# A scan that feeds an expert layer: the first steps, the end of the scan, the gates and the PSUM tiles are reordered

## The chip, the cores and the metric

The kernel runs on one core of a Trainium2 chip. The metric is the device time of one execution in microseconds. The engines are called by the names that the profile uses: PE (TensorE, with its weight loads as PEld), DVE (VectorE), ACT (ScalarE), POOL (GpSimd) and SP (SyncE, which issues most DMAs). A lower time is better.

## The reference

Two layers follow one another. The first is a scan with decay over 768 positions of 4 sequences with 8 heads (head size 32, state size 16), in chunks; the second sends each of the 3072 resulting rows of 256 numbers to one of 8 experts.

```
for each chunk of the sequence:
    L  = exp(cum_i - cum_j), causal            # cum = cumulative sum of log(a) inside the chunk
    y  = ((C B^T) * L) x  +  exp(cum) * (C state)
    state = exp(sum log a) * state + sum_j exp(cum_last - cum_j) * B_j x_j
x = y as [3072, 256]
logits = (x/|x|) . (emb/|emb|) / tau           # cosine router, 8 experts
gate   = softmax(logits)[argmax]
out[r] = gate[r] * relu(x[r] w1[e]) w2[e],  e = argmax(logits[r])   # w1: 256x1024, w2: 1024x256
```

## The kernel before, in words

The order in which the program is written is the order of each engine's queue (`manual_schedule`): nothing is moved afterwards. Engines wait for one another through semaphores only where one needs what another makes, or a buffer that another still uses. PSUM, into which PE writes, has eight banks; the kernel names them `pgA`, `pgB`, `py` (two banks each) and `pz0`, `pz1` (one each) and uses the same five tiles in the scan and in the experts.

**The scan** works on 6 chunks of 128 positions, and on each in two steps of two sequences, so there are 12 steps. Ahead of them `decays` (DVE) makes the decay factors, `spread_decays` (L214, PE) copies those of a chunk from 32 rows to all the rows that need them, by a product with a 0/1 matrix, and ACT brings them to SBUF as `fr`; `inverse` and `turn_inverse` make the reciprocals `rT`. `embeddings` norms the experts' vectors (L268) and `turn_embeddings` turns them. A step is made of `scores` (L430: C times the decay, `cp`, against B, split by `split_b` into the two heads of a row group, `bz`, L157 on ACT), `masks` (a copy on ACT, L440, a product on DVE, L441, a selection on POOL, L447), `outputs` one step later (L462 from the state, L471 from the scores), `tokens` another step later (L520: the row and its logits), and `keep_tokens` (ACT copy to `yt`, L531, and a DMA to the table `rows` in HBM). Every second step makes the new state (`sums`, `states`). `scale_c` (DVE) and `scale_x` (POOL, for the first chunk DVE) prepare a chunk ahead.

**The routing** runs beside it, per chunk: `pick` finds the expert of each token, `ranks` counts by small products where each comes in its expert's list, `places` makes two 0/1 patterns `low` and `hv` from it (L367), and `table` and `keep_table` (L374, L383) add to a table of row numbers per expert. Of expert 0 the first 256 rows are taken from chunks 0 to 3 alone, so `early_rows` can gather them before the scan has ended; it issues the gather of job 0 (L637, on POOL).

**The experts** are nine jobs: job 0 (256 early rows of expert 0), job 1 (160 more), jobs 2 to 8 (416 rows each, experts 1 to 7). A job is a gather of its rows (L637; four instructions for 416 rows), `turn_x` (transposes L675 and copies L677), eight `up` (L685: 2 products each, 4 instructions in the profile; relu by turns on ACT L689 and DVE L691), `gates` (squares on ACT L655, a pow on POOL L658, five short steps on DVE, an exp on ACT L662), `down` (L699: two halves of 8 products each, 16 instructions in the profile; copies on ACT L703 and DVE L705) and `out` (transposes L713, scaling by the gate on ACT L719 and DVE L717, scatter L720 on POOL). `up` takes three banks in turn, the input transposes one, `down` two, the output transposes two. The jobs overlap by one: `out` of job n stands behind the second `up` of job n+1, and the gather of job n+2 behind `down` of job n. In job 4 `left_blocks` (L809 to L860, mostly DVE) computes where rows beyond 416 would go; there are none, and `leftover` runs no loop.

Of the kernel before, what the change touches and what calls it, by code (L numbers as in the profile page):

```python
# [7 lines left out]
F32 = mybir.dt.float32  # L8
# [38 lines left out]
def early_consts(k):  # L47
# [5 lines left out]
    g.iota(head_i[:], pattern=[[NH, NB], [1, 4], [4, 2], [0, N]], base=0, channel_multiplier=0)  # L53
    v.memset(k.a0[64:128, 1, :], 1.0)
# [98 lines left out]
def split_b(k, c):  # L153
    t = k.ld[c]
    t.bz = k.work.tile([128, 2, NB, Q], F32, name="bz", tag="bz")
    for v in range(2):
        k.nc.scalar.activation(t.bz[:, v], t.bt[:], ACT.Copy, scale=k.tmask[:, v : v + 1])  # L157
# [9 lines left out]

def decays(k):  # L170
# [23 lines left out]
    v.tensor_tensor(out=k.f[:, :, HQ], in0=w[:, 0], in1=at[:, :, 0], op=ALU.mult)  # L194

# [10 lines left out]
def spread_at(k, c):  # L206
    return (k.py[:, 0], k.py[:, 1], k.pz[0], k.pz[1], k.pgA[:, 0], k.pgA[:, 1])[c]


def spread_decays(k, c):  # L210
    g = 32 * (c % 4)
    ps = spread_at(k, c)
    for b in range(NB):
        k.nc.tensor.matmul(  # L214
            ps[:, 128 * b : 128 * b + 128], lhsT=k.spread[g : g + 32, b, :], rhs=k.f[g : g + 32, c // 4, :],
            start=True, stop=True, tile_position=(g, 0),
        )
# [39 lines left out]
def embeddings(k):  # L257
# [7 lines left out]
    nc.scalar.dma_start(tau[:], k.tau.to_broadcast([E, 1]))  # L265
    sq = k.mc.tile([E, DM], F32, name="emb_sq")
# [13 lines left out]
def turn_embeddings(k, ps):  # L280
# [5 lines left out]
    nc.vector.tensor_copy(out=k.turn[:, 0, LG : LG + E], in_=ps[:, 0:E])  # L286
    nc.vector.tensor_copy(out=k.turn[:, 1, 0:E], in_=ps[:, E : 2 * E])
# [18 lines left out]
def ranks(k, c):  # L306
    nc = k.nc
    ob = k.ob[c]
    at = k.pz[1][:, AT : AT + NB * E].rearrange("p (b e) -> p b e", b=NB)
# [10 lines left out]
    if c in (3, NC - 1):  # L320
        n = k.pz[1][:, CNT : CNT + E]
# [48 lines left out]
def table(k, c):  # L370
    nc = k.nc
    ps = k.pz[0][:, TB : TB + 2 * E * NT]
# [6 lines left out]
def keep_table(k, c):  # L379
    nc = k.nc  # L380
    ps = k.pz[0][:, TB : TB + 2 * E * NT]
    acc = k.acc[:].rearrange("p v m -> p (v m)")
    nc.vector.tensor_tensor(out=acc, in0=acc, in1=ps, op=ALU.add)  # L383
# [142 lines left out]
def keep_tokens(k, p):  # L526
    nc = k.nc
    c, b, _ = pair(k, p)
# [8 lines left out]
def mamba(k):  # L537
# [3 lines left out]
    early_consts(k)  # L541
    load(k, 0)
# [7 lines left out]
    for c in (0, 4, 5, 1, 2, 3):  # L550
        spread_decays(k, c)
    flat = lambda c: k.fr[:, c].rearrange("p b m -> p (b m)")
    nc.scalar.copy(out=flat(0), in_=spread_at(k, 0))
    nc.vector.memset(k.fr[:, 0, :, HQ], 1.0)
    nc.scalar.copy(out=k.fr[:, 4:6].rearrange("p c b m -> p c (b m)"), in_=k.pgA[:])
    scale_c(k, 0)
    scale_c(k, 1)
    inverse(k, 0)
    scores(k, 0)
    for c in (1, 2, 3):  # L560
        nc.scalar.copy(out=flat(c), in_=spread_at(k, c))
    turn_inverse(k, 0, k.py[:, 0, 0:128])
    k.rT = k.mc.tile([128, 2, 128], F32, name="rT")
    nc.scalar.copy(out=k.rT[:, 0], in_=k.py[:, 0, 0:128])
    scale_x(k, 0, nc.vector)
    scale_x(k, 1, nc.vector)
    masks(k, 0)
    inverse(k, 1)
    between(k)
    turn_inverse(k, 1, k.py[:, 0, 0:128])  # L570
    nc.scalar.copy(out=k.rT[:, 1], in_=k.py[:, 0, 0:128])
    turn_embeddings(k, k.pz[0])
    split_b(k, 1)
    scale_c(k, 2)
    load(k, 2)

    for s in range(1, NP + 2):
# [13 lines left out]
        if s % 2 and s >= 5:  # L591
# [406 lines left out]
```

## Time and profile before

| | |
|---|---|
| median of 3 runs | 373.27 us (370.19 to 374.04) |
| the profiled execution | 374.36 us, of which the trace spans 372.6 us |
| mean granted clock of PE | 0.917 |
| busy | PE 289.9, PEld 181.1, DVE 115.4, ACT 84.3, POOL 105.7 us |
| start to the first scores of step 2 | 25.14 us |
| from there to the scores of step 11 | 45.64 us |
| from there to the first matmul of job 2 | 69.94 us |
| from there to the first `down` product of job 8 | 204.11 us |
| the rest | 27.77 us |

The time of an execution is 1.76 us more than its span here. The page gives busy times of the whole span; the stretches are read with the view by windows, which gives busy times and the clock of PE for each. In a group or timeline row, the number in brackets is how long the engine stood still ahead of the instruction, and the name behind `<-` is what released it. In the waits view a row has the total, the times and the longest. A matmul that is written once appears as two instructions in the profile, since the numbers are float32.

### The profile page before, as it was taken

Reading aid. Unit: us, or ns where it says so; the run is one execution under the profiler, and the core shown is the slowest. Engines: PE = TensorE matmul, PEld = TensorE weight load, DVE = VectorE, ACT = ScalarE, POOL = GpSimd, SP = SyncE. Lnnn points to the kernel's source line nnn. Section 1 sums busy time; section 2 is a strip of 40 time slices with the busy share of each in tenths; the row PEclk is TensorE's granted clock in tenths of the full one; section 3 lists DMA queues with packets and bytes.
Section 4 is the critical chain, followed back from the end, with each engine's and each line's share of the span. In section 5 each row is a group of like instructions: output and inputs, shape, how many; then the busy total and the mean of one; then the engine's idle time right before and its main releaser. Section 6 shows DMA issues by size and latency. Waiting matters only on the chain.

```text
span 372.6 us, 5520 instructions
## 1 busy us (share of the span) xinstructions
PE 289.9 (78%) x2159; PEld 181.1 (49%) x2159; DVE 115.4 (31%) x356; ACT 84.3 (23%) x210; POOL 105.7 (28%) x130
## 2 busy tenths in 40 slices
PE   3777879857549689798889799497988996898940
PEld 3666768744327675344345354234444453454420
DVE  3476767861320312302211220812033023122010
ACT  3445555530100203101301300130031022013010
POOL 4334453430420523401800810260035022014030
PEclk9999999995857969989999899869999999999995
DMA  6506692831110144503232230413043240001010
GB/s 212 221 4 201 203 360 99 270 107 29 32 27 0 43 140 131 155 3 113 73 125 90 85 130 0 128 59 131 0 151 82 83 138 14 0 0 46 0 41 7
DMA packets 20428, 34.76 MB, mean 93 GB/s; under 512 B 2232, under 2 KB 13700, under 8 KB 20400
## 3 DMA queue, kind: packets, MB, share of 16 engines
q1 hardware_dynamic: 17360, 27.94, 22.1%
q0 software_dynamic: 2816, 6.40, 5.8%
q8 instruction: 17, 0.28, 0.3%
q14 instruction: 11, 0.09, 0.1%
q10 hardware_dynamic: 224, 0.06, 0.1%
HBM read 28.26 MB, written 6.65 MB: 94 GB/s over the span
## 4 chain that ended last, share of the span: by engine, by line
PE 59%; issue 10%; DVE 7%; ACT 7%; POOL 4%; DMA 2%; POOLq 0%; DVEq 0%; ACTq 0%
PE py L699 23%; PE pgA L685 16%; PE pgB L685 6%; PE pgB L675 3%; PE py L471 2%; PE pz L520 2%; ACT hT L689 2%; PE pgA L430 2%; DVE hT L691 2%; POOL gr L658 2%; PE pz L713 2%; PE py L462 1%; POOL out_dram L720 1%; DVE xT L677 1%; ACT bz L157 1%
## 5 line engine op out<-in xcount | busy, mean ns | idle before, releaser
L699 PE MATMUL py<-hT,w 128*128 128x416 f32 (+2 forms) x288 | 99.0, 500 | 5.0 <-ACT yoT L703 5.0
L685 PE MATMUL pgA<-xT,w 128*128 128x416 f32 (+2 forms) x192 | 79.6, 543 | 25.8 <-ACT hT L689 21.7
L699 PEld LDWEIGHTS py<-hT,w 128*128 128x128 f32 x288 | 55.1, 202 | 44.4 <-issue 32.5
L720 POOL DMA_INDIRECT out_dram<-yo,to x30 | 29.2, 975 | 165.7 <-ACT yo L719 155.4
L685 PEld LDWEIGHTS pgA<-xT,w 128*128 128x128 f32 x192 | 37.8, 215 | 59.0 <-ACT hT L689 31.7
L637 POOL DMA_INDIRECT xg<-rows,table x30 | 30.1, 1002 | 21.3 <-DVE to_u L402 13.2
L685 PE MATMUL pgB<-xT,w 128*128 128x416 f32 (+2 forms) x96 | 35.9, 499 | 0.0
L705 DVE COPY yoT<-py 128x416 f32<-128x416 f32 (+2 forms) x9 | 4.9, 543 | 99.2 <-PE py L699 87.7
L691 DVE TENSOR_SCALAR hT<-pgA 128x416 f32<-128x416 f32 (+2 forms) x24 | 12.9, 536 | 57.0 <-PE pgA L685 47.2
L689 ACT ACTIVATE hT<-pgA 128x416 f32<-128x416 f32 (+2 forms) x24 | 11.5, 478 | 67.8 <-PE pgA L685 67.8
L685 PEld LDWEIGHTS pgB<-xT,w 128*128 128x128 f32 x96 | 18.9, 205 | 13.1 <-issue 12.7
L447 POOL TENSOR_SCALAR_AFFINE_SELECT g<-g 128x1024 f32<-128x1024 f32 x12 | 13.5, 1123 | 37.4 <-ACT g L440 35.8
L675 PE MATMUL pgB<-ident,xg 128*128 128x128 f32 x64 | 13.7, 309 | 11.8 <-DVE xT L677 6.1
L703 ACT COPY yoT<-py 128x416 f32<-128x416 f32 (+2 forms) x9 | 4.2, 467 | 80.2 <-PE py L699 80.2
L430 PE MATMUL pgA<-cp,bz 32*128 32x128 f32 x192 | 16.9, 313 | 6.4 <-ACT bz L157 5.2
L675 PEld LDWEIGHTS pgB<-ident,xg 128*128 128x128 f32 x64 | 8.6, 155 | 19.8 <-DVE xT L677 7.3
L430 PEld LDWEIGHTS pgA<-cp,bz 32*128 32x128 f32 x192 | 13.7, 209 | 8.2 <-ACT bz L157 7.0
L430 PE MATMUL pgB<-cp,bz 32*128 32x128 f32 x192 | 16.9, 312 | 0.0
L713 PE MATMUL pz<-ident,yoT 128*128 128x128 f32 (+1 forms) x64 | 10.9, 285 | 7.6 <-DVE yo L717 4.5
L441 DVE TENSOR_TENSOR g<-pgA,mask 128x1024 f32<-128x1024 f32 x12 | 14.6, 1216 | 2.4 <-PE pgB L430 2.4
L520 PE MATMUL pz<-turn,yT 128*128 128x136 f32 x96 | 14.6, 293 | 0.1
L440 ACT COPY g<-pgB 128x1024 f32<-128x1024 f32 x12 | 12.1, 1006 | 8.6 <-PE pgB L430 7.5
(184 smaller groups left out, 294.0 us busy)
## 6 DMA issues: line engine op xcount, KB each, us to landing
w<-in_moe_w_dram SPq DMA_DIRECT2D x16, 1024.0 KB, 5.6
rows<-yt SPq DMA_DIRECT2D x12, 264.0 KB, 3.7
x<-in_x_dram SPq DMA_DIRECT2D x6, 512.0 KB, 5.5
ct<-in_CT_dram SPq DMA_DIRECT2D x6, 256.0 KB, 3.0
bt<-in_BT_dram SPq DMA_DIRECT2D x6, 256.0 KB, 4.2
b<-in_B_dram SPq DMA_DIRECT2D x6, 256.0 KB, 6.5
xg<-rows,table POOLq DMA_INDIRECT x30, 2.8
out_dram<-yo,to POOLq DMA_INDIRECT x30, 2.4
```

Of the source, the lines that this page charges most:

```text
L430: k.nc.tensor.matmul((k.pgA, k.pgB)[q // 2][:, q % 2, a : a + 128], lhsT=t.bz[r, v, b + i, :], rhs=t.cp[r, b + i, :], start=True, stop=Tru ...
L441: nc.vector.tensor_tensor(out=s.g[:, 0:2].rearrange("p q a i -> p (q a) i"), in0=k.pgA[:].rearrange("p q (a i) -> p (q a) i", a=4), in1=bc ...
L447: nc.gpsimd.affine_select(out=g, in_=g, pattern=[[0, 8], [1, Q]], compare_op=ALU.is_ge, fill=0.0, base=0, channel_multiplier=-1)
L520: k.nc.tensor.matmul(k.pz[i][:, at : at + Y1], lhsT=yT[:, j, i, :], rhs=k.turn[:, j, :], start=(j == 0), stop=(j == 1), skip_group_check=True,
L637: s.k.nc.gpsimd.indirect_dma_start(out=s.x[0:p, i, 0:TOK], out_offset=None, in_=rows, in_offset=bass.IndirectOffsetOnAxis(ap=s.at[0:p, i : ...
L675: nc.tensor.transpose(t[:, o : o + p], s.x[0:p, i, Y1 * j : Y1 * j + 128], k.ident[:p, :p])
L685: nc.tensor.matmul(t, lhsT=s.w1[:, j, 128 * f : 128 * f + 128], rhs=s.xT[:, j, :], start=(j == 0), stop=(j == KD - 1))
L689: nc.scalar.activation(s.hT[:, f, :], t, ACT.Relu)
L691: nc.vector.tensor_scalar_max(s.hT[:, f, :], t, 0.0)
L699: nc.tensor.matmul(t, lhsT=s.w2[:, f, 128 * j : 128 * j + 128], rhs=s.hT[:, f, :], start=(f == 0), stop=(f == KF - 1))
L713: nc.tensor.transpose(t[:p, 128 * j : 128 * j + 128], s.yT[:, j, o : o + p], k.ident[:])
L720: d = nc.gpsimd.indirect_dma_start(out=k.out[:, :], out_offset=bass.IndirectOffsetOnAxis(ap=s.to[0:p, i : i + 1], axis=0), in_=y[:p], in_o ...
```

## The change

The change has five parts.

1. **First steps.** A tile of zeros and a first `Square` on ACT come at the very start; nine products with zeros (`fill`) stand on PE ahead of and behind the first spread. The spread of chunks 0 to 3 goes over the four row groups in turn (chunk within block, where it was block within chunk), that of chunks 4 and 5 comes after the scores of step 0. `scale_c` of the first two steps reads PSUM. Norm and turn of the embeddings come after the masks of step 0, their copies go from DVE to ACT, and the second `inverse` moves to steps 3 and 4. The scores and masks of steps 0 and 1 are written out in `begin_scan`.
2. **B split sooner.** `split_b` of the next chunk moves from the odd step to the even step before it.
3. **End of the scan.** `table(3)`, its addition and `early_rows` move into step 11: the products behind the scores, the rest behind the masks. The last steps are written out.
4. **Experts.** Eight tiles of one bank each come from a pool of their own, with `reuse_waits="tile"`. `gates` is split into `squares` (with the pow) and the rest; for job n+1 both stand between the two halves of `down` of job n, and the gather of job n+2 between them. `left_blocks` stands in front of the second half of `down` of job 4. In job 0 the relus of `up` 0 to 5 are all on ACT, and `gates` and the gathers are reordered.
5. **A drain** of POOL stands behind the scatter of job 7, in the last expert.

The core of the diff:

```diff
+def fill(k, n):
+    for _ in range(n):
+        k.nc.tensor.matmul(k.pgB[:, 1, 0:Q], lhsT=k.zero[:, 0:Q], rhs=k.zero[:, Q:], start=True, stop=True)
...
-def spread_decays(k, c):
-    g = 32 * (c % 4)
-    ps = spread_at(k, c)
+def spread_decays(k, chunks):
     for b in range(NB):
...
+        for c in chunks:
+            g = 32 * (c % 4)
...
-    for c in (0, 4, 5, 1, 2, 3):
-        spread_decays(k, c)
...
+    spread_decays(k, range(4))
     inverse(k, 0)
+    fill(k, 1)
+    turn_inverse(k, 0, k.pgB[:, 1, 0:128])
...
+    keep_decays(k, 1)
...
+    scale_c(k, 0, spread_at(k, 0))
     scores(k, 0)
...
+    scale_c(k, 1, spread_at(k, 0))
     scale_x(k, 0, nc.vector)
+    keep_decays(k, 2)
+    masks(k, 0)
+    spread_decays(k, (4, 5))
+    keep_decays(k, 4)
+    keep_decays(k, 5)
     scale_x(k, 1, nc.vector)
...
+    scores(k, 1)
+    keep_decays(k, 3)
     between(k)
...
+    norm_embeddings(k)
+    masks(k, 1)
     turn_embeddings(k, k.pz[0])
...
             scores(k, s)
+            if s == NP - 1:
+                table(k, 3)
             masks(k, s)
...
+            if s == NP - 1:
+                keep_table(k, 3)
+                early_rows(k)
...
+        if s % 2 == 0 and s // 2 + 1 < NC:
+            split_b(k, s // 2 + 1)
...
-        if s % 2 and c + 1 < NC and s > 1:
-            split_b(k, c + 1)
...
+    def squares(s):
...
+        nc.gpsimd.tensor_tensor(out=s.r[:], in0=s.r[:], in1=k.half[:, 0:nt], op=ALU.pow)
...
+    banks = [k.ps.tile([128, 512], F32, name=f"bank{i}") for i in range(8)]
+    k.bank = {"hp": ring(banks[0:3]), "xt": ring(banks[3:4]), "yp": ring(banks[4:6]), "ot": ring(banks[6:8])}
...
+    j0.up(6)
+    j0.up(7)
+    load_weights(k, 2)
+    j0.down(0)
+    j0.squares()
     begin(1)
     j0.gates()
...
+    j0.down(1)
     jobs[1].turn_x()
...
+    jobs[1].squares()
+    jobs[1].gates()
     for n in range(1, E + 2):
...
                 jobs[n - 1].out()
-            if f == 3 and n <= E:
-                jobs[n].gates()
+                if n == E:
+                    k.nc.gpsimd.drain()
         if n + 1 <= E:
             jobs[n + 1].turn_x()
         if n <= E:
-            jobs[n].down()
+            jobs[n].down(0)
+        if n + 1 <= E:
+            jobs[n + 1].squares()
         if 2 <= n + 1 < E:
             begin(n + 1)
+        if n + 1 <= E:
+            jobs[n + 1].gates()
+        if n == E // 2:
+            left_blocks(k)
+        if n <= E:
+            jobs[n].down(1)
```

Line numbers move: the scores are L430 before and L453 after, the table's products L374 and L397, the relu on ACT L689 and L740, the squares L655 and L695, the exp L662 and L713, the pow L658 and L699, the gather L637 and L684, the scatter L720 and L772.

Three places show how the instructions stand. The first is PE at the end of the scan: the last scores (step 11), and what follows them. Before:

```order
L430 MATMUL pgA<-cp,bz 128x128 x2
L430 MATMUL pgB<-cp,bz 128x128 x2
L462 MATMUL py<-cp,T 32x128 x16
L471 MATMUL py<-g,xs 32x128 x16
L520 MATMUL pz_74<-turn,yT 128x136 x2
L520 MATMUL pz_75<-turn,yT 128x136 x2
L374 LDWEIGHTS low
L374 MATMUL pz_74<-hv,low 128x64
```

After:

```order
L453 MATMUL pgA<-cp,bz 128x128 x2
L453 MATMUL pgB<-cp,bz 128x128 x2
L397 LDWEIGHTS low
L397 MATMUL pz_87<-hv,low 128x64
L397 LDWEIGHTS low
L397 MATMUL pz_87<-hv,low 128x64
L397 LDWEIGHTS low
L397 MATMUL pz_87<-hv,low 128x64
L397 LDWEIGHTS low
L397 MATMUL pz_87<-hv,low 128x64
L485 MATMUL py<-cp,T 32x128 x16
```

The table's products of chunk 3 (`hv`, `low`) have moved from behind the outputs and tokens of step 10 to the place right behind the scores; the outputs (L462, now L485) stand behind them.

The second is ACT in an expert. Here `hT<-` are the relus of `up`, `yoT<-` is the copy of the first half of `down`, `yo<-` the output scaling, and the `bank_` numbers are the eight one-bank tiles (1372 to 1374 for `up`, 1376 for the first half of `down`, 1378 for the outputs). Before, an expert from the output scaling to the next job's first relu:

```order
L719 ACTIVATE yo<-pz_74,gate 128x256 x2
L689 ACTIVATE hT<-pgA 128x416
L655 ACTIVATE sq,gr<-xg_179 128x256 x4
L662 ACTIVATE gl<-gl 128x32
L689 ACTIVATE hT<-pgA 128x416
L689 ACTIVATE hT<-pgB 128x416
L703 COPY yoT<-py 128x416
L689 ACTIVATE hT<-pgA 128x416
```

After:

```order
L771 ACTIVATE yo<-bank_1378,gate 128x256 x2
L740 ACTIVATE hT<-bank_1374 128x416
L740 ACTIVATE hT<-bank_1373 128x416
L740 ACTIVATE hT<-bank_1372 128x416
L755 COPY yoT<-bank_1376 128x416
L695 ACTIVATE sq,gr<-xg_181 128x256 x4
L713 ACTIVATE gl<-gl 128x32
L740 ACTIVATE hT<-bank_1374 128x416
```

The squares and the exp (`gl`) stood between two relus of the same job. Now they are the next job's, behind the copy of the first half of `down`, and the next relu is the first of the next job.

The third is POOL at the first jobs: gathers (`xg`), pows (`gr`) and scatters (`out_dram`). Before:

```order
L637 DMA xg_178<-rows,early_i 128x264 x2
L637 DMA xg_179<-rows,table 128x264
L637 DMA xg_179<-rows,table 32x264
L637 DMA xg_180<-rows,table 128x264 x3
L637 DMA xg_180<-rows,table 32x264
L658 TENSOR_TENSOR gr<-gr,half 128x2
L720 DMA out_dram<-yo,early_to 3072x256 x2
L658 TENSOR_TENSOR gr<-gr,half 128x2
```

After:

```order
L684 DMA xg_180<-rows,early_i 128x264 x2
L684 DMA xg_181<-rows,table 128x264
L684 DMA xg_181<-rows,table 32x264
L699 TENSOR_TENSOR gr<-gr,half 128x2
L684 DMA xg_182<-rows,table 128x264 x3
L684 DMA xg_182<-rows,table 32x264
L699 TENSOR_TENSOR gr<-gr,half 128x2
L772 DMA out_dram<-yo,early_to 3072x256 x2
```

The pow of job 0 has moved ahead of the four gathers of job 2; that of job 1 stands behind them and ahead of the scatter of job 0.

More of the change, by code (lines that the diff above doesn't have):

```diff
@@ L150, in load, with split_b @@
     nc.sync.dma_start(t.b[:].rearrange("p b m -> p (b m)"), k.B[c])
-def split_b(k, c):
+def split_b(k, c, halves=(0, 1)):
     t = k.ld[c]
-    t.bz = k.work.tile([128, 2, NB, Q], F32, name="bz", tag="bz")
-    for v in range(2):
+    if 0 in halves:
+        t.bz = k.work.tile([128, 2, NB, Q], F32, name="bz", tag="bz")
+    for v in halves:
         k.nc.scalar.activation(t.bz[:, v], t.bt[:], ACT.Copy, scale=k.tmask[:, v : v + 1])
@@ L651, in gates @@
         )
-        r = k.p.tile([128, nt], F32, name="gr", tag="gr")
-        for i in range(nt):
-            sq = k.p.tile([128, 2, 128], F32, name="sq", tag="sq")
-            nc.scalar.activation(
-                sq[:], x[:, i].rearrange("p (j w) -> p j w", j=2)[:, :, 0:128], ACT.Square, accum_out=r[:, i : i + 1],
-            )
-        nc.gpsimd.tensor_tensor(out=r[:], in0=r[:], in1=k.half[:, 0:nt], op=ALU.pow)
         nc.vector.tensor_scalar_add(r[:], r[:], 1e-6)
@@ L691, in up, with down @@
             nc.vector.tensor_scalar_max(s.hT[:, f, :], t, 0.0)
-    def down(s):
+    def down(s, j):
         k, nc = s.k, s.k.nc
-        s.yT = k.p.tile([128, KD, s.w], F32, name="yoT", tag="yoT")
-        for j in range(KD):
+        if j == 0:
+            s.yT = k.p.tile([128, KD, s.w], F32, name="yoT", tag="yoT")
+        for j in (j,):
             t = k.bank["yp"]()[:, 0 : s.w]
@@ L937 @@
     k.route = ctx.enter_context(tc.tile_pool(name="route", bufs=2))
-    ps = ctx.enter_context(tc.tile_pool(name="ps", bufs=1, space=PSUM))
-    k.pgA = ps.tile([128, 2, 512], F32, name="pgA")
-    k.pgB = ps.tile([128, 2, 512], F32, name="pgB")
-    k.py = ps.tile([128, 2, 512], F32, name="py")
-    k.pz = [ps.tile([128, 512], F32, name=f"pz{i}") for i in range(2)]
     k.yt = k.const.tile([128, NU, TOK], F32, name="yt")
@@ L950 @@
             k.mc = m.enter_context(tc.tile_pool(name="mc", bufs=1))
+            ps = m.enter_context(tc.tile_pool(name="ps", bufs=1, space=PSUM))
+            k.pgA = ps.tile([128, 2, 512], F32, name="pgA")
+            k.pgB = ps.tile([128, 2, 512], F32, name="pgB")
+            k.py = ps.tile([128, 2, 512], F32, name="py")
+            k.pz = [ps.tile([128, 512], F32, name=f"pz{i}") for i in range(2)]
             mamba(k)
         k.p = ctx.enter_context(tc.tile_pool(name="moe", bufs=2, reuse_waits="tile"))
+        k.ps = ctx.enter_context(tc.tile_pool(name="moe_ps", bufs=1, space=PSUM, reuse_waits="tile"))
         moe(k)
```

181 lines of the change are left out of this document (99 added, 82 removed).

## The prediction

> **What bounds the kernel now.** I read the page first, then stretches of the span, then the waits, then the timeline where the long waits lie. The page:
>
> ```profile
> PE 289.9 (78%) x2159; PEld 181.1 (49%) x2159; DVE 115.4 (31%) x356; ACT 84.3 (23%) x210; POOL 105.7 (28%) x130
> PEclk9999999995857969989999899869999999999995
> ```
>
> TensorE (PE) is busy for 78% of the span. The rest is 82.7 us in which it waits, and some of the busy time is matmuls at the half clock (the fives in the second row). So I ask of each stretch how long PE stands and at which clock. The columns are length, busy time of PE, PEld, DVE, ACT and POOL, the granted clock, DMA share and GB/s. The cuts are at the first scores of step 2 (25.14), those of step 11 (70.78), the first transpose of job 0 (85.10), the end of its long stall (106.53), the first matmul of job 2 (140.72), and then the first down matmul of jobs 4 (220.09), 5, 6, 7 and 8.
>
> ```profile
> 0.00:25.14 25.14, 15.21 (x180) 14.04 (x180) 11.19 (x39) 9.97 (x17) 7.96 (x33) 1.00 0.46 161
> 25.14:70.78 45.64, 38.25 (x1073) 32.32 (x1066) 34.09 (x84) 26.05 (x47) 23.43 (x23) 1.00 0.59 201
> 70.78:85.10 14.32, 8.63 (x202) 7.13 (x198) 8.85 (x41) 5.13 (x12) 3.89 (x4) 0.90 0.54 181
> 85.10:106.53 21.43, 11.43 (x40) 7.62 (x41) 5.78 (x27) 2.33 (x9) 6.60 (x7) 0.66 0.11 28
> 106.53:140.72 34.19, 28.90 (x121) 23.20 (x122) 6.25 (x22) 3.63 (x13) 6.83 (x7) 0.76 0.15 50
> 220.09:258.14 38.05, 29.93 (x82) 15.10 (x81) 12.09 (x42) 5.34 (x16) 8.98 (x9) 0.87 0.27 87
> 258.14:288.22 30.08, 26.31 (x82) 13.38 (x81) 6.15 (x17) 5.22 (x16) 9.00 (x9) 1.00 0.27 84
> 288.22:317.95 29.73, 25.43 (x81) 13.62 (x81) 6.34 (x17) 5.22 (x16) 4.99 (x5) 1.00 0.22 81
> 344.83:372.60 27.77, 12.92 (x41) 6.61 (x39) 2.14 (x4) 1.45 (x3) 3.88 (x4) 0.81 0.05 16
> ```
>
> The expert rows are bound by PE (25.4 of 29.7 us); the rows from 70.78 to 140.72 are not, and run at 0.66 to 0.90 of the clock. The waits view names what PE stands for (total us, times, longest):
>
> ```profile
> PE pgA L685 <- ACT hT L689: 21.7, 15, 8.1
> PE py L699 <- ACT yoT L703: 5.0, 9, 0.6
> PE pgA L430 <- ACT bz L157: 5.2, 4, 1.4
> ```
>
> An up matmul waits for the relu that frees its PSUM bank; ScalarE (ACT) is late with the relu because the gate's exp is ahead of it in its queue, and that waits for VectorE (DVE), which waits for the pow on GpSimd (POOL). The timeline of job 0 shows the whole chain, the worst of its kind:
>
> ```profile
> 103.67 0.91 POOL L637 DMA_INDIRECT xg<-rows,table  x1 [0.30 <-issue]
> 104.61 0.74 POOL L658 TENSOR_TENSOR gr<-gr,half 128x2 f32<-128x2 f32 x1
> 105.99 0.21 ACT L662 ACTIVATE gl<-gl 128x16 f32<-128x16 f32 x1 [10.11 <-DVE gl L661]
> 106.53 2.07 PE L685 MATMUL pgA<-xT,w 128*128 128x256 f32 x4 [8.13 <-ACT hT L689]
> ```
>
> The pow stands behind the last of six gathers (five of them at 0.30 us from the one before), and PE loses 8.13 us.
>
> **The change, part by part.** *Start.* Timeline rows:
>
> ```profile
> 5.62 2.07 PE L214 MATMUL py<-f,spread 32*128 32x128 f32 x8 [5.62 <-DVE f L194]
> 5.76 1.28 ACT L268 ACT_TABLE_LOAD   x1 [5.76 <-DMA tau<-in_moe_tau_dram]
> 11.88 2.08 PE L214 MATMUL pz<-f,spread 32*128 32x128 f32 x12
> 12.16 0.58 ACT L553 COPY fr<-py 128x512 f32<-128x512 f32 x1 [3.37 <-PE py L214]
> 13.72 0.58 PE L430 MATMUL pgA<-cp,bz 32*128 32x128 f32 x2
> ```
>
> The decays are ready at 5.62, but the spread of chunks 0, 4, 5, 1, 2, 3 runs chunk after chunk to 12.16, and the copy for `scale_c` waits for it. Before, twelve products on mixed row groups took 2.08 us; the sixteen for chunks 0 to 3, now dealt over four groups, should take no more than 2.1, so they end at 7.7. The table load no longer waits for tau, so the first B halves are done by then, and `scale_c` reads PSUM without the copy (0.58). With 0.4 us for it scores(0) start at 8.3, 5.4 sooner than 13.72. From there to scores(2) 11.4 us passed (to 25.14). New ACT copies (chunks 1, 2, 4, 5, 3 one by one, the turn table) and the embedding chain, which now stands between the first two steps, can take some of it back. I take −4.5, with bounds −2 (the chain becomes late) and −6.5 (the distance shrinks too). The nine fill products are before 5.6, where PE had nothing.
>
> *Scan.* Four stalls of 1.4 us for `bz` (5.2 in all) go, because the split is issued a step sooner, ahead of its use by about five us. DVE is next: it is busy 34.1 of 45.6 us and the chain mask, scale, states is late by about as much. I take −1.5, bounds 0 and −3.
>
> *End of the scan, jobs 0 and 1 (70.78 to 140.72, 69.94 us).* PE's work at the full clock is 8.63×0.90 + 11.43×0.66 + 28.90×0.76 = 37.3 us. It stood 69.94 − 48.96 = 21.0 us. What remains of that: the gather of job 0 hung on keep_table(3), which moves ahead of outputs(10):
>
> ```profile
> 81.41 1.32 POOL L637 DMA_INDIRECT xg<-rows,early_i  x1 [5.54 <-DVE early_to_u L403]
> 85.15 0.47 PE L675 MATMUL pgB<-ident,xg 128*128 128x128 f32 x1 [3.87 <-DMA xg<-rows,early_i]
> 73.41 0.40 ACT L367 ACTIVATE hv<-hi,part 128x128 bf16<-128x128 f32 x1 [2.13 <-DVE hi L360]
> ```
>
> The `hv` of chunk 3 is ready at 73.8; with the products (0.3), the add after the mask on DVE (to 75.1) and the indices (0.4) the gather goes out about 75.9, 5.5 sooner. The wait for `hv` now also holds outputs(10) for up to 1.5 us, so the transposes come only 3.8 sooner: 5.7 − 3.8 = 1.9 us stay in the first row. In the second the 8.13 goes, since pow of job 0 is now ahead of the four gathers of job 2 and relus 0 to 5 ahead of the exp: 10.0 − 8.1 = 1.9 stay. What is late next is job 1: its exp waits for a pow behind those four gathers (1.3 us apart, 5.2), of which about 3.6 lie beside down(1) and the transposes; 1.6 is left, and 1.6 of small waits in the third row. Sum 7.0, so 44.3; I add 2.6 for one or two half-clock windows (next part). 46.9, thus −23.0. Bounds: −27 at the full clock and with no stall in job 1; −17 if its stall is the whole 5.2 and two more windows are half.
>
> *Experts 2 to 8 (140.72 to 344.83, 204.11 us).* Rows of one undisturbed expert:
>
> ```profile
> 294.60 5.85 PE L699 MATMUL py<-hT,w 128*128 128x416 f32 x16 [0.60 <-ACT yoT L703]
> 300.29 1.56 PE L685 MATMUL pgB<-xT,w 128*128 128x416 f32 x4
> 303.08 0.60 PE L713 MATMUL pz<-ident,yoT 128*128 128x128 f32 x4
> 304.55 1.56 PE L685 MATMUL pgA<-xT,w 128*128 128x416 f32 x4
> 306.56 0.41 ACT L655 ACTIVATE sq<-xg 128x256 f32<-128x256 f32 x1
> ...
> 311.51 1.66 PE L685 MATMUL pgA<-xT,w 128*128 128x416 f32 x4 [2.61 <-ACT hT L689]
> 315.81 0.66 PE L675 MATMUL pgB<-ident,xg 128*128 128x128 f32 x4
> 317.23 0.72 PE L675 MATMUL pgB<-ident,xg 128*128 128x128 f32 x4 [0.75 <-DVE xT L677]
> 317.88 2.36 PE L699 MATMUL py<-hT,w 128*128 128x416 f32 x6
> ```
>
> By starts: half of a down 5.69 (294.60 to 300.29), one up 1.39 (two from 300.29 to 303.08), the output transposes 1.47 (to 304.55), the input transposes 2.07 (315.81 to 317.88). Without the 2.61 (gates) and the 0.60 (second half waits for the copy of the first, which before shared a two-bank tile) a period is 2×5.69 + 8×1.39 + 1.47 + 2.07 = 26.1. The gates' cover is now the second half of down: after the copy (0.5) come four squares (4×0.41), the pow (0.74 in job 0, for half the columns; I take 1.0), three short DVE steps and the exp (0.21): with the hand-overs about 3.8 us, under 5.69. If that slips by over 2 us, the next relu is late by the rest. The block table (L809 to L860, on DVE) keeps its price: the row at 220.09 is 38.05 − 30.08 = 8.0 longer, and as its step now stands ahead of the copy of the second half, the output transposes still wait for it, by 4 us or so. Bounds 3.7 (the wait alone) and 9. Six periods less the transposes that job 8 doesn't issue: 154.6; up to the first down of job 2 (8 ups, two output blocks, transposes) 14; the block table 8; one half-clock window 1.7. Sum 178.3, so −25.8, bounds −19 and −28.
>
> The clock has rows of its own:
>
> ```profile
> 153.90:157.30 3.40, 2.03 (x10) 1.19 (x10) 1.48 (x3) 0.00 (x0) 0.00 (x0) 1.00 0.65 172
> 157.30:160.70 3.40, 3.40 (x6) 1.69 (x5) 0.30 (x1) 0.00 (x0) 0.00 (x0) 0.50 0.34 140
> ```
>
> A stretch of 3.4 us in which PE was busy for 2.0, 1.45 of them in the eight transposes of job 3, was followed by one at half, which costs 1.7. [...]
>
> *Tail.* The first scatter of the last job, and the drains at the kernel's end (count, shortest, median and longest in ns, first and last start):
>
> ```profile
> 358.91 1.05 POOL L720 DMA_INDIRECT out_dram<-yo,to  x1 [19.05 <-ACT yo L719]
> L994 POOLq DRAIN  x3: 46/107/5301, 366.5 to 372.4; - x3
> ```
>
> One drain of 5.30 us runs near the end, from 366.5, and two others take 0.11 and 0.05. The early drain stands where POOL is idle for 19.05 us, waiting for the last job's outputs, so it costs nothing there. If its price belongs to what was queued since the start, or to the first drain, the last falls to the level of the other two: −5.0. If it belongs to the last scatters, 0. Both ends stay in the range; I take −5.0, nearer the rows of the two cheap drains. With the 0.6 of down: −5.6.
>
> Sum: 372.6 − 4.5 − 1.5 − 23.0 − 25.8 − 5.6 = 312.2. The profiled execution took 374.36, 1.76 more than its span, so 314; it lies 1.1 above the median 373.27, which gives 313.
>
> **The rivals.** *Half clock more often.* With fewer waits the transposes (2.07 and 1.47 us per expert) become the thin places; if every expert from 2 to 8 has one half window, that adds six more, 6×1.7 = 10, so 323. For: 157.30, where transposes alone did it. Against: the row at 288.22 has the same transposes, and a wait of 2.61, at 1.00. [...]
>
> *The last drain stays.* +5: 318. For: it is what POOL does behind the last scatters, and theirs could be the cost. Against: POOL issues one of these in 1.05 us, and 5.30 for four of them that are under way already would be more than their issue took.
>
> *The gates' wait moves.* If pow is late (ACT's squares and the scatters are in front of it), the exp holds relu 0 of the next expert, by what it was before: 7×2.6 = 18, so 331.
>
> *Start and scan give nothing, DVE being the bound:* 313 + 6 = 319, and with the bound of the middle (6 less) 325.
>
> *Slower.* The same queue, at its worst: the exp of job n+1 stands ahead of relu 0 on ACT and its DVE steps ahead of the copy of the second down half. If x of n+1 or the pow came as late as in job 0, PE would lose 8.13 plus 3.4 of half clock behind it, 11.5 per expert, 81 in all: 394. It decides from 60/7 = 8.6 per expert. Against: the gathers of n+1 are now issued a whole expert ahead, and four gathers take 5.2, not 7.8.
>
> **How the numbers follow.** Forecast as summed 0.42; half clock 0.18; drain stays 0.16; gates move 0.08; start and scan give nothing 0.10; slower 0.03; about no change, several of these together, 0.03. The likeliest gives 313. The low end, 303, takes the good bounds of the middle and the experts (−4, −2.2) and most of the start's and scan's (−3.5); the high end, 331, takes in all rivals but the last two cases, and the bound of the middle. Within 1%, about what a measurement of this kernel can tell from no change, is 369.5 to 377: 0.03; slower 0.03; faster 0.94.
>
> **What would show it.** Scores(2) at 19 to 22 us; no wait for `bz` over 0.5; the first gather 5 us after scores(11); no PE wait over 3 us between job 0 and job 2; expert periods of 26 to 27 with no wait of L685's line for ACT over 1 us and none of the down line; the clock row at 9 through the experts except the block table; the drain near the end under 1 us, and one of about 5 us at the last expert where POOL waits. The forecast is wrong if the periods stay at 29, if pow is late again, or if the five in the clock row come with every expert.

## The result, and the profile after

The changed kernel takes 314.25 us in the median of four runs (310.73 to 315.82), against 373.14 before: a ratio of 0.840, with a 95% interval of 0.832 to 0.847. The forecast was 313, with a range of 303 to 331. Ratios, here and below, are taken from the faster of two states into which the executions of a kernel fall, so they can differ a little from the quotients of the medians. The page of its profiled execution (314.79 us, span 313.1), as far as it answers to the rows shown of before:

```profile
PE 270.8 (87%) x2177; PEld 178.2 (57%) x2177; DVE 115.2 (37%) x352; ACT 86.3 (28%) x217; POOL 105.8 (34%) x130
PEclk9558999995999799999999999779999999999997
L736 PE MATMUL bank<-xT,w 128*128 128x416 f32 (+2 forms) x288 | 96.7, 489 | 2.0 <-ACT hT L740 2.0
L751 PE MATMUL bank<-hT,w 128*128 128x416 f32 (+2 forms) x288 | 91.7, 476 | 0.0
```

The last two rows are the up and down products; what stands behind the second bar is PE's idle time ahead of them: 2.0 us and none, where the waits for the relu alone were 21.7 and those for the first down half 5.0. The clock row has no fives left in the experts; three stand elsewhere, two in the start and one at the end of the scan. The stretches, cut at the same events as before (scores of step 2 at 21.26, of step 11 at 70.00, first matmul of job 2 at 115.49, first down product of job 8 at 292.00; two single experts between):

```profile
0.00:21.26 21.26, 14.13 (x198) 12.82 (x198) 12.42 (x40) 10.03 (x20) 10.66 (x35) 0.71 0.54 191
21.26:70.00 48.74, 40.78 (x1066) 34.26 (x1066) 33.20 (x85) 26.63 (x48) 21.32 (x20) 0.95 0.58 194
70.00:115.49 45.49, 40.09 (x359) 34.25 (x359) 20.43 (x88) 13.43 (x44) 12.90 (x13) 0.89 0.29 93
115.49:292.00 176.51, 163.17 (x518) 90.11 (x517) 46.98 (x138) 34.77 (x102) 57.12 (x58) 0.98 0.30 94
155.04:180.97 25.93, 24.90 (x82) 13.79 (x81) 6.27 (x17) 5.35 (x16) 9.01 (x9) 1.00 0.35 110
180.97:216.23 35.26, 27.08 (x82) 14.79 (x81) 12.19 (x42) 5.36 (x16) 9.17 (x10) 0.90 0.27 84
292.00:313.10 21.10, 12.65 (x41) 6.72 (x39) 2.14 (x4) 1.45 (x3) 3.82 (x4) 0.91 0.06 21
```

| stretch | before | after | difference | forecast |
|---|---|---|---|---|
| start to scores of step 2 | 25.14 | 21.26 | −3.9 | −4.5 |
| to scores of step 11 | 45.64 | 48.74 | **+3.1** | −1.5 |
| to the first matmul of job 2 | 69.94 | 45.49 | −24.5 | −23.0 |
| to the first down product of job 8 | 204.11 | 176.51 | −27.6 | −25.8 |
| to the end | 27.77 | 21.10 | −6.7 | −5.6 |

The sum is −59.5, the forecast was −60.4. The scan went the other way. The first rows of the two kernels can't be compared by their clocks: before, the row reads 1.00, but the scores of steps 0 and 1 take 2.16 and 2.17 us in it, and 1.17 in step 2; after, they take 2.09 where the trace has the clock at 0.50 (9.11 to 26.18 us). Two further things in the trace were not as the terms had them. The expert with the block table is 35.26 long, 9.3 more than its neighbour. Its timeline:

```profile
195.28 0.17 POOL L870 IOTA step_i<- 128x32 int32 x1
195.48 0.18 DVE L872 CAST step_f<-step_i 128x32 f32<-128x32 int32 x1 [3.85 <-POOL step_i L870]
202.03 0.58 DVE L757 COPY yoT<-bank 128x416 f32<-128x416 f32 x1
202.66 2.16 PE L765 MATMUL bank<-ident,yoT 128*128 128x128 f32 x7 [7.36 <-DVE yoT L757]
```

The first instruction of the table is a small iota on POOL, which now stands behind the four gathers of job 6. DVE waits 3.85 us for it, and the copy of the second down half, with PE behind it, waits for the whole. The granted clock is 0.50 from 200.25 to 207.08, around the end of this wait.

And the scan's waits of PE (total, times, longest; whole span):

```profile
PE py L494 <- issue: 4.2, 3, 1.7
PE pgA L453 <- DVE g L464: 2.3, 3, 1.0
```

The 5.2 us for `bz` are gone; in their place are waits for the mask on DVE, and 4.2 us in which PE waited for nothing that the profile shows (0.95 before).

### The profile page after: what moved, and what is told of

It reads as the page before. It is cut to its first block, busy times and chain, and to the rows that moved or that the text cites. A ratio compares the mean times of both kernels' runs of the same rounds, so it can differ in the third digit from the quotient of the medians.

```text
span 313.1 us, 5513 instructions
## 1 busy us (share of the span) xinstructions
PE 270.8 (87%) x2177; PEld 178.2 (57%) x2177; DVE 115.2 (37%) x352; ACT 86.3 (28%) x217; POOL 105.8 (34%) x130
## 4 chain that ended last, share of the span: by engine, by line
issue 55%; PE 17%; POOL 16%; DVE 8%; ACT 1%; POOLq 1%; DMA 1%; ACTq 0%; DVEq 0%
POOL out_dram L772 8%; POOL xg L684 7%; PE py L494 4%; PE pz L543 3%; PE pgA L453 3%; PE bank L736 2%; PE py L485 1%; DVE g L464 1%; DVE cp L253 1%; DVE T L533 1%; PE py L225 1%; PE pz L512 1%; DMA a<-in_a_dram 1%; POOL gr L699 1%; ACT fr L232 1%
## 5 line engine op out<-in xcount | busy, mean ns | idle before, releaser
L736 PE MATMUL bank<-xT,w 128*128 128x416 f32 (+2 forms) x288 | 96.7, 489 | 2.0 <-ACT hT L740 2.0
L751 PE MATMUL bank<-hT,w 128*128 128x416 f32 (+2 forms) x288 | 91.7, 476 | 0.0
L736 PEld LDWEIGHTS bank<-xT,w 128*128 128x128 f32 x288 | 54.5, 199 | 37.4 <-issue 33.7
L751 PEld LDWEIGHTS bank<-hT,w 128*128 128x128 f32 x288 | 52.5, 190 | 34.9 <-issue 33.7
L772 POOL DMA_INDIRECT out_dram<-yo,to x30 | 29.2, 974 | 42.5 <-ACT yo L771 35.5
L742 DVE TENSOR_SCALAR hT<-bank 128x416 f32<-128x416 f32 (+2 forms) x33 | 18.3, 554 | 63.0 <-PE bank L736 60.8
L699 POOL TENSOR_TENSOR gr<-gr,half 128x4 f32<-128x4 f32 (+1 forms) x9 | 8.7, 972 | 95.7 <-ACT sq L695 95.7
L684 POOL DMA_INDIRECT xg<-rows,table x30 | 30.2, 1008 | 21.6 <-DVE to_u L425 13.5
L740 ACT ACTIVATE hT<-bank 128x416 f32<-128x416 f32 (+2 forms) x39 | 18.1, 470 | 65.1 <-PE bank L736 60.4
L453 PE MATMUL pgA<-cp,bz 32*128 32x128 f32 x192 | 17.0, 326 | 5.0 <-DVE cp L253 2.7
L494 PE MATMUL py<-g,xs 128*32 128x128 f32 x384 | 16.9, 313 | 4.2 <-issue 4.2
L765 PE MATMUL bank<-ident,yoT 128*128 128x128 f32 (+1 forms) x64 | 11.4, 298 | 10.2 <-DVE yoT L757 7.9
L453 PEld LDWEIGHTS pgA<-cp,bz 32*128 32x128 f32 x192 | 14.4, 225 | 6.3 <-DVE g L464 2.7
L726 PE MATMUL bank<-ident,xg 128*128 128x128 f32 x64 | 11.5, 273 | 6.6 <-DVE xT L728 6.1
L453 PE MATMUL pgB<-cp,bz 32*128 32x128 f32 x192 | 17.1, 328 | 0.0
L494 PEld LDWEIGHTS py<-g,xs 128*32 128x32 f32 x384 | 12.0, 124 | 7.8 <-issue 7.5
```

What stands on the lines that cost most here:

```text
L453: k.nc.tensor.matmul((k.pgA, k.pgB)[q // 2][:, q % 2, a : a + 128], lhsT=t.bz[r, v, b + i, :], rhs=t.cp[r, b + i, :], start=True, stop=Tru ...
L494: nc.tensor.matmul(k.py[g : g + 32, v, 128 * i : 128 * i + 128], lhsT=t.xs[:, b + i, 4 * v + q, :], rhs=s.g[:, q, 2 * i + v, :], start=(c ...
L684: s.k.nc.gpsimd.indirect_dma_start(out=s.x[0:p, i, 0:TOK], out_offset=None, in_=rows, in_offset=bass.IndirectOffsetOnAxis(ap=s.at[0:p, i : ...
L736: nc.tensor.matmul(t, lhsT=s.w1[:, j, 128 * f : 128 * f + 128], rhs=s.xT[:, j, :], start=(j == 0), stop=(j == KD - 1))
L740: nc.scalar.activation(s.hT[:, f, :], t, ACT.Relu)
L742: nc.vector.tensor_scalar_max(s.hT[:, f, :], t, 0.0)
```

## The experiments

Twelve kernels were run, in three groups, each beside runs of the kernel before on the same chip (medians 374.3, 376.0 and 374.0). Ratios are to those runs; the changed kernel has 0.840.

**1. No drain.** The two lines `if n == E: k.nc.gpsimd.drain()` are taken out of the changed kernel.

> The changed kernel without the drain in the last expert. If the price of the last drain belongs to what was queued since the start (the prediction), the drain at the end goes back from 0.38 to about 5.3 us and the time rises by 4.9, to 319. If the early drain only moved a wait for landings that would be over anyway, the drain at the end stays under 1 us and the time stays at 314.

321.2 us, ratio 0.857 (0.849 to 0.864). The drains at the end, with the drain (first row) and without:

```profile
L1055 POOLq DRAIN  x3: 46/107/380, 311.5 to 312.8; - x3
```

```profile
L1053 POOLq DRAIN  x3: 46/107/5301, 312.3 to 318.2; - x3
```

4.92 us of drain come back, and the span is 5.3 longer. The drain is worth what the forecast took.

**2. Gates in their old place.** In the changed kernel, squares and gates of job n go back behind its own `up(3)`, the next gather behind the whole of down; the one-bank tiles stay.

```diff
+            if f == 3 and n <= E and n > 1:
+                jobs[n].squares()
+                jobs[n].gates()
...
-        if n + 1 <= E:
-            jobs[n + 1].squares()
-        if 2 <= n + 1 < E:
-            begin(n + 1)
-        if n + 1 <= E:
-            jobs[n + 1].gates()
         if n == E // 2:
             left_blocks(k)
         if n <= E:
             jobs[n].down(1)
+        if 2 <= n + 1 < E:
+            begin(n + 1)
```

> The changed kernel with squares and gates of jobs 2 to 8 back in the middle of their own ups, and the next gather behind the whole of down, as before the change; the one-bank tiles stay. By the prediction PE again waits about 2.6 us for a relu in each of jobs 2 to 8, behind the exp, so 7 x 2.6 = 18 us more: 332. If the one-bank tiles alone made the periods short, the wait is under 1 us and the time at most 318.

313.5 us, ratio 0.837 (0.830 to 0.843): no slower than the changed kernel. Two periods, the second with the block table:

```profile
152.50:178.50 26.00, 24.97 (x81) 13.69 (x80) 6.22 (x17) 5.23 (x16) 9.05 (x11) 1.00 0.33 111
178.50:204.50 26.00, 24.97 (x81) 13.70 (x80) 12.07 (x42) 5.23 (x16) 9.13 (x10) 1.00 0.34 112
```

And the timeline in one of them, where the old wait of 2.6 us would be:

```profile
168.02 8.29 PE L736 MATMUL bank<-xT,w 128*128 128x416 f32 x23
174.31 0.23 ACT L713 ACTIVATE gl<-gl 128x32 f32<-128x32 f32 x1 [2.58 <-DVE gl L712]
174.44 0.50 ACT L740 ACTIVATE hT<-bank 128x416 f32<-128x416 f32 x1
```

ACT still stands 2.58 us with the exp, and its relu is late by that. PE doesn't notice: its 23 instructions run through. So the late relu was not moved away by the change; it stopped mattering. The block table, ahead of whose iota there are no gathers in this order, costs nothing. The one price of the old place is in job 8: its pow is behind the drain, and PE waits 4.9 us for a relu there.

**3. Two-bank tiles.** In the changed kernel the banks of up, input transposes and down are halves of three tiles again.

```diff
-    banks = [k.ps.tile([128, 512], F32, name=f"bank{i}") for i in range(8)]
+    two = [k.ps.tile([128, 2, 512], F32, name=f"two{i}") for i in range(3)]
+    banks = [two[i // 2][:, i % 2] for i in range(6)] + [k.ps.tile([128, 512], F32, name=f"bank{i}") for i in range(2)]
```

> The changed kernel with six of the eight one-bank PSUM tiles of the experts taken as halves of three two-bank tiles, as before the change. By the prediction the second half of each down waits 0.6 us for the copy of the first: 9 x 0.6 = 5 us more, 319. If waits follow the bank and not the tile, no row changes and the time stays at 314. If the ups' shared tile counts too, 0.6 more for each up that finds its neighbour's relu running, two or three per expert: 325 to 330.

341.2 us, ratio 0.912 (0.904 to 0.920). One period and PE's waits in it:

```profile
231.60:261.20 29.60, 26.01 (x81) 13.43 (x80) 6.27 (x17) 5.35 (x16) 8.98 (x9) 1.00 0.26 87
```

```profile
PE two L736 <- ACT hT L740: 1.2, 2, 0.6
PE two L726 <- DVE xT L728: 0.8, 1, 0.8
PE two L736 <- DVE hT L742: 0.7, 1, 0.7
PE two L751 <- ACT yoT L755: 0.6, 1, 0.6
```

With the gates a layer ahead, but tiles of two banks, a period is as long as before the change (29.6 against 29.7). An up waits 1.2 us for relus on ACT and 0.7 for one on DVE, where the changed kernel's period (155.04 to 180.97) has no such wait: with a shared tile it also waits until the relu has read the other half. This is the dearest part to undo: 27 us, more than any of the three outcomes expected.

**4. B split late.** In the changed kernel `split_b` goes back to the odd step.

> The changed kernel with the B split back in the odd step. Theory one, VectorE bounds the scan: the waits for bz (1.4 us each) come back, the waits of the odd scores for the mask go, and the time from the scores of step 2 to those of step 11 stays within 1 us of 48.7; 314. Theory two (the prediction): the move was worth 1.5 to 3 us, so 316 to 317. Theory three, the move made the scan longer because the split is ahead of something on ScalarE that VectorE needs: 45.6 us for the scan and 311.

314.2 us, ratio 0.834 (0.826 to 0.842). The waits for `bz` are back and the scan takes as long:

```profile
PE pgA L453 <- ACT bz L162: 5.2, 4, 1.4
```

From the scores of step 2 to those of step 11 it takes 49.24 us, against 48.74. Step by step: from odd to even scores 5.44 and 5.84 instead of 4.28 and 4.40, from even to odd 5.23 and 4.33 instead of 5.65 and 6.22 (steps 3 to 7). What the earlier split gives to one kind of step the other kind takes: steps 3 to 7 take 20.83 us with the late split and 20.54 with the early one. Theory one stands. But the scan isn't at 45.6 either, so the loss against before is not the split's.

**5. One-bank tiles alone.** The kernel before, with six one-bank tiles in a pool of their own in the experts and nothing else.

> The kernel before with one part of the change alone: six one-bank PSUM tiles in the experts instead of three two-bank tiles; gates, gathers and everything else stay where they were. Theory now (from the two runs that undid the gates' place and the tiles, 313.5 and 341.2): the tiles carry the whole gain of the experts, since the up may run three banks ahead of a late relu. Then the periods fall from 29.7 to about 26 with the gates in their old place, and the time by 24 to 28, to 347 to 350. Prediction's theory, the gates' place carries it: only the 0.6 waits go, 366.

337.5 us, ratio 0.903 (0.896 to 0.910): more than expected. A period is 26.0, with the gates where they were:

```profile
175.00:201.00 26.00, 24.97 (x81) 13.71 (x80) 6.16 (x17) 5.23 (x16) 9.02 (x10) 1.00 0.35 111
```

From job 2 to job 8 the experts take 173.9 us, 2.6 less than in the changed kernel, where the block table costs 9.3 and here 6.3 (32.30 against 26.00). The stretch from step 11 to job 2 is 61.9, 8 shorter than before, though one wait of 7.7 for the relu remains there: three banks, by an estimate from two starts of before (96.41 and 97.38) 1.0 us each at 256 columns, are used up long before the six gathers are issued, which took 7.4 us before (97.19 to 104.58).

**6. The pow of job 0 first, alone.** The kernel before, with `j0.gates()` ahead of `begin(1)`.

> The kernel before with one line moved: the gates of job 0 ahead of the four gathers of job 2, so that their pow stands ahead of these. By the prediction the 8.13 us stall goes and some half clock with it: 362 to 366. Rival: the pow still waits behind the two gathers of job 1 and the stall only shrinks to 2 or 3 us, with the gathers late instead: 369 to 372.

368.3 us, ratio 0.991 (0.985 to 0.997): closer to the rival. The pow now follows the two gathers of job 1 only:

```profile
98.20 0.94 POOL L637 DMA_INDIRECT xg<-rows,table  x1 [0.30 <-issue]
99.17 0.74 POOL L658 TENSOR_TENSOR gr<-gr,half 128x2 f32<-128x2 f32 x1
100.09 1.09 POOL L637 DMA_INDIRECT xg<-rows,table  x1 [0.18 <-POOL gr L658]
101.09 1.33 PE L685 MATMUL pgA<-xT,w 128*128 128x256 f32 x4 [2.99 <-ACT hT L689]
```

The stall falls from 8.13 to 2.99. In the trace job 2 begins 61.5 us after step 11 instead of 69.9, and nearly 2 us of that are lost again before job 8. The times credit the run with less than its trace: the ratio is worth 3.2 us (1.0 to 5.5).

**7. Block table first.** In the changed kernel `left_blocks(k)` moves ahead of the next job's squares, so ahead of the gathers too.

> The changed kernel with the block table of job 4 ahead of the next job's squares and gates instead of behind them. Theory: the 7.4 us wait of the output transposes comes from the table standing on VectorE between the gates' last step and the copy of the second half of down; started some 4 us sooner it ends before that half does, and the time falls by 8 to 9, to 305 to 306. Rival: the gates are late instead and hold the first relu of job 5; the gain is under 3, 312.

304.6 us, ratio 0.825 (0.819 to 0.831). The medians give the expected gain, 9.7 us; the ratios give 5.6. The period with the table is now like its neighbours:

```profile
177.20:203.10 25.90, 24.87 (x81) 13.78 (x80) 12.19 (x42) 5.35 (x16) 8.99 (x9) 1.00 0.35 113
```

The order on DVE was only a part of the cause; the iota behind the gathers was the other. The run moves both at once and doesn't tell their shares.

**8. First weights late.** The first two loads of weights move from steps 5 and 9 to steps 9 and 11.

> The changed kernel with the first two loads of expert weights moved from steps 5 and 9 of the scan to steps 9 and 11. Theory one: the waits of PE that the profile calls issue (4.2 us in the scan, 0.95 before) come from transfers that fill the DMA engines between 40 and 60 us; without the weights there they fall under 1.5 us and the scan from 48.7 to about 46: 311 to 312. Theory two: they belong to places in the program, and stay at 2 to 4 us: 314.

312.3 us, ratio 0.844 (0.838 to 0.849). The waits that the profile calls issue (in the stretch of the scan):

```profile
PE py L494 <- issue: 2.9, 2, 2.3
```

They don't go; in run 2, with the loads in their old place, they are shorter (1.9). The time and the scan (46.8 us) lie nearer to theory one, but with the loads in their old place the same scan takes 45.4 to 48.6 us (runs 1, 2, 3, 7 and 10), so they don't decide. In the changed kernel the waits stand behind PE's 730th, 858th and 985th matmul of the recorded ones, 127 or 128 apart; in runs 1, 2, 7 and 9 to 12 at the same three, in run 8 at the 730th and the 985th, in run 3 at the 475th and the 985th, in run 4, run 6 and the kernel before at the one next to 858 alone, in run 5 there and at the 475th. Their length changes from run to run (0.5 to 2.4 us). So they belong to places in the program, not to those transfers. What else moves at these times can be read from the traces. The page of the changed kernel has this queue:

```profile
q8 instruction: 17, 0.28, 0.4%
```

That is 17 packets of 16 KB, one for every 256 of PE's 4354 recorded matmuls and weight loads, and the three places lie 256 and 254 of these apart. The three waits of the changed kernel, 0.94, 1.67 and 1.56 us long, end 2.40, 2.34 and 2.50 us after a packet of this queue starts; the one of the kernel before, 0.95 long, ends 2.46 after. In the 14 traces there are 33 such waits of over 0.4 us at these places. In 31 of them PE goes on 2.25 to 2.65 us after a packet of this queue starts, and in the two others, where the packet itself takes over 2 us instead of about 1, after 3.5 to 3.7. That PE waits there for what these packets bring is the author's reading of these times; no run moves the packets, so it is not shown.

**9. A faster version.** Run 7, with the input transposes alternating over two banks, the output transposes over three, and the turn of the embeddings behind the first outputs.

```diff
-    "xt": ring(banks[3:4]), ... "ot": ring(banks[6:8])
+    "xt": ring([banks[3], banks[7]]), ... "ot": ring([banks[6], banks[7], banks[3]])
```

> A version meant to beat both: the block table ahead of the gates (304.6 alone), the input transposes alternating over two banks and the output transposes over three (the changed kernel waits 0.68 us per expert for the copy of the first half of x, and 0.35 for an output bank), and the turn of the embeddings behind the first outputs instead of ahead of them (PE waits 2.2 us for it). If these waits are on the path: 8 x 0.68 + 7 x 0.35 = 8 us less for the banks and 2 for the turn, 294 to 296. If the scan's chain takes the 2 us back: 297. If the banks only move the waits to the next copy on VectorE: 302 to 305.

297.6 us, ratio 0.799 (0.792 to 0.805).

```profile
151.80:176.70 24.90, 24.77 (x82) 13.82 (x81) 6.30 (x18) 5.32 (x16) 9.22 (x10) 1.00 0.37 117
176.70:201.60 24.90, 24.77 (x82) 13.82 (x81) 12.20 (x43) 5.31 (x16) 9.01 (x9) 1.00 0.37 117
```

PE stands for 0.1 us of 24.9. By the medians it is 7 less than run 7, by the ratios 10, where 10 were hoped for; in the trace 1.0 per expert came. The turn gave at most 0.7 of its 2.2 (scores of step 2 at 20.58), since they then wait 2.6 for `cp` on DVE.

**10. Drain behind job 5.** The early drain moves two jobs forward.

> The changed kernel with the early drain behind the outputs of job 5 instead of job 7. Theory one: a drain costs a price for each gather or scatter queued on GpSimd since the last one (5.30 us for 64 without the early drain, 4.97 and 0.38 for 60 and 4 with it, 0.083 each). Then this one takes about 4.0 for 48 and the last 1.3 for 16, and the time is 1 longer, 315, unless the pow behind it is late. Theory two, the first drain pays once: the last stays at 0.4.

314.2 us, ratio 0.843 (0.836 to 0.850). The last drain:

```profile
L1055 POOLq DRAIN  x3: 46/107/1362, 310.4 to 312.3; - x3
```

1.36 us for the 16 gathers and scatters behind the early one, 0.085 each. Theory one had 1.3. The early drain of the changed kernel itself, with the last scatter ahead of it:

```profile
287.26 0.89 POOL L772 DMA_INDIRECT out_dram<-yo,to  x1 [0.30 <-issue]
L838 POOLq DRAIN  x1: 8222/8222/8222, 284.9 to 284.9; - x1
```

From the end of that scatter (288.15) to the end of the drain (293.12) it is 4.97 us, for 60. In run 10 the same distance at its early drain is 4.00 us (234.92 to 238.92), for 48, as theory one had it. The microsecond that the time should have lost (315) doesn't show in 314.2.

**11. End of the scan as before.** `table(3)`, its addition and `early_rows` go back behind the places of chunk 4.

> The changed kernel with part three undone: table 3, its addition and the early gather go back to where they stood, behind the outputs and tokens of step 10 and the places of chunk 4. By the prediction the first transposes come 3.8 us later and the whole by as much: 318. Rival: job 0 waits later for the last places anyway and gives all but 1 us of it back: 315.

318.7 us, ratio 0.849 (0.838 to 0.860); the trace is of an execution of 319.9, the longest of the four. The first gather of job 0, with the changed order and with this one:

```profile
74.94 1.32 POOL L684 DMA_INDIRECT xg<-rows,early_i  x1 [0.52 <-DVE early_to_u L426]
```

```profile
82.93 1.32 POOL L680 DMA_INDIRECT xg<-rows,early_i  x1 [7.18 <-DVE early_to_u L426]
```

From the scores of step 11 that is 4.9 and 11.6 us; the first transposes come 11.8 and 14.8 behind them, and job 2 begins 3.7 later. The interval of the time alone (it overlaps the changed kernel's) would not settle it. The traces do: in runs 1, 4, 7, 10 and 12, which keep this part of the change, job 2 begins 43.0 to 45.9 us after the scores of step 11, here 49.2.

**12. Spread chunk by chunk.** `spread_decays(k, (c,))` for each of the first four chunks, instead of all four dealt out.

> The changed kernel with the sixteen first spread products chunk after chunk instead of dealt over the four row groups. By the prediction the dealing is what makes the first scores early: one row group takes 0.21 us a product, so they end 2.2 us later (16 x 0.21 against 1.17) and scores of step 0 start at 11.2 instead of 9.05; 316. Rival: the reciprocal on VectorE, or the chain to the scores of step 2, hides it: 314.

316.9 us, ratio 0.848 (0.840 to 0.856), which overlaps the changed kernel's. In the trace (of an execution of 319.25, the longest of the four) the scores of step 0 start at 13.29 instead of 9.05 and those of step 2 at 25.51 instead of 21.26. But these 4.2 us are not all due to the dealing. The last rows of the spread in the changed kernel, in run 2 (dealt as well) and in this run:

```profile
6.88 0.28 PE L225 MATMUL pz<-f,spread 32*128 32x128 f32 x2
```

```profile
7.62 0.43 PE L225 MATMUL pz<-f,spread 32*128 32x128 f32 x2
```

```profile
8.69 2.29 PE L225 MATMUL pz<-f,spread 32*128 32x128 f32 x13
```

The first began at 5.99, the second at 5.96, the third at 5.85: 1.17, 2.09 and 5.13 us for the same 32 instructions. One of them takes 0.27 us in the first trace and 0.42 in the two others, so PE was slower there. Three of the runs with dealt products began at the slower pace (2, 4 and 11); their scores of step 0 start at 10.24 to 10.36 and those of step 2 at 22.46 to 22.57. Against these the dealing is worth 3.0 us, and the faster pace of the changed kernel's trace the other 1.2. The expected 2.2 set sixteen products of 0.21 us against 1.17, the time of the other pace; here, chunk after chunk, a product takes 0.32 (5.13 for sixteen).

## Why the prediction was right, and where it wasn't

**The total and the range** held, 314.25 against 313, and so did the tail, the start and the stretch of the first jobs to within 1.5 us each. Part of that is luck: the scan's miss of +4.6 and the start's of +0.6 were nearly paid by −1.5, −1.8 and −1.1 in the three stretches behind them. (The period adds up to 26.04, where the forecast has 26.1; that moves its total by 0.4.)

**Start: right in size, the cause shown in part.** Run 12 against runs 2, 4 and 11 shows that dealing the products over the row groups is worth 3.0 us. The step that gave its price was misread: the x12 of the row for 2.08 us counts instructions, so it is six products, and the sixteen are 32. They took 1.17 us or 2.09, by PE's pace, so that 2.1 held is luck. That pace changed from run to run with the same program: the scores of step 2 start at 21.15 to 22.70 in the changed kernel and in runs 1, 2, 3, 4, 7, 8, 10 and 11, those of the old start at 25.14 to 26.22 in the kernel before and runs 5 and 6, so the start is worth 2.4 to 5.1. What the nine products with zeros do for it, no run tests.

**Scan: wrong.** The step that failed is "I take −1.5, bounds 0 and −3". That DVE is next in line is what run 4 bears out, and it leaves 0.3 us for the earlier split in steps 3 to 7. The sum has no term for what the scan can lose. By the starts of the scores, the 3.1 us are lost in four places. From step 2 to 3 it takes 5.50 against 4.13 before (1.4 lost): step 2 runs at half clock here (its scores take 2.09 where later ones take 1.17), and in runs 8 and 10, where they take 1.17, the same code needs 3.2. From 7 to 9 it takes 12.27 against 11.32 (0.95 lost): two of the issue waits lie there, 3.2 us together, and in run 2, where they are 1.3, the same steps take 10.34. From 3 to 7 0.6 are lost; there stands the second inverse with its turn, which the change moves out of the start and to which the forecast gave no price. From 9 to 11 it is 0.2. So most of the loss is no fixed price of the change: the same scan takes 45.36 to 48.55 us in runs 1, 2, 3, 7 and 10, and the old one 44.99 to 47.26 in the kernel before and runs 5 and 6. That step 2 could run at half the clock was not argued, and why its scores take 1.17 us in some runs and 2.09 here stays open.

**End of the scan and first jobs: right size, mixed cause.** In the traces, each alone: one-bank tiles 8, the pow of job 0 first 8, the early gather 3.7. The three make 20 of the 24.5, with 2 to 3 us of scatter (see run 11), and the times give the pow only 3.2; the forecast gave the tiles nothing here. The late pow of job 1 came as said: 2.0 us of wait against 1.6.

**Experts: right size, wrong cause.** The step that failed is "Without the 2.61 (gates) and the 0.60 …", where the first was put down to the gates' move and the second alone to the tiles. Run 2 has the gates in their old place and no 2.61; run 3 has them moved and a period of 29.6; run 5 has the tiles alone and a period of 26.0. The waits row named the relu that PE waited for, and the chain behind it was read rightly; what was not asked is how far PE could run ahead of a late relu. Three banks, at 1.39 us an up, cover a relu that is 2.58 late (run 2); halves of shared tiles don't (2.61 of wait in the kernel before). The move of the gates gave nothing and cost the block table's 9.3, which run 7 gets back. The forecast had 8.0 for it and saw its place on DVE, but not the iota behind the gathers on POOL, for which DVE waits 3.85 us: the queue of a second engine past which the step was moved.

**The clock.** The half window allowed for did not come in the experts without the block table: the rows at 25.93 (the changed kernel) and 26.00 (run 2) are at 1.00, though their transposes are those of before. That speaks against the rival with a half window in every expert, too. The one row below 1.00 in the experts from job 2 on, 0.90, is the one with the wait of 7.36 us; there the clock was 0.50 for 6.8 us. Before, it was 0.50 from 157.30 to 160.70, with no wait of PE over 0.7 us from 150 to 157.30. What made it fall there no run shows.

**Drain: right**, by the times of run 1 (5.30 us for 64 queued transfers), the changed kernel (4.97 for 60, 0.38 for 4) and run 10 (4.00 for 48, 1.36 for 16).

**The other rivals.** The gates' wait didn't move to a later place in the steady state; in run 2 it shows once, behind the drain. The slower case never came near: the largest wait behind a relu was 2.0 us.

## What to carry to other kernels

Where PE waits for whoever frees its PSUM, ask first how many outputs it may run ahead, and whether the wait is tied to a tile that is larger than the output (a period took 29.6 us with tiles of two banks and 25.9 with tiles of one); only then what makes the other engine late. A step that is moved is to be priced where it arrives, on every engine that it issues to: a single iota behind four gathers held DVE for 3.85 us, in a wait of PE of 7.36. And a sum that comes out right is no proof of its terms; the runs that undo one part each gave another cause for the largest of them.

## What was not expected of the hardware

- The last drain of POOL took 5.30 us with 64 indirect transfers queued since the start (run 1), 1.36 with 16 since the drain before it (run 10) and 0.38 with 4 (the changed kernel); the early drain ended 4.97 us behind the last scatter with 60 queued and 4.00 with 48 (run 10). From 16 on that is 0.083 to 0.085 us for each, though most of them were issued long before.
- In the changed kernel PE stood still three times in the scan, with its many short products, for 0.94, 1.67 and 1.56 us, 256 and 254 recorded matmuls and weight loads apart, where the profile shows nothing that it waits for; it went on 2.40, 2.34 and 2.50 us after the start of a 16 KB packet of the queue called instruction. In the 14 traces these stops took 0.5 to 2.4 us, not at each of the places in each run, and 31 of 33 ended 2.25 to 2.65 us after such a start. With two loads of weights moved away (run 8) two of them, 2.9 us together, are still there.
- Sixteen float32 products (32 instructions) that read different row groups in turn ran in 2.09 us (run 2), and in 5.13 chunk after chunk at the same pace of PE (run 12); at the faster pace of the changed kernel's trace they ran in 1.17.
